# An attention-and-MLP block on one core: the order of the first normalizations, and which loads wait for which work

## The chip, the cores and the metric

The kernel runs on one core of one Trainium2 chip. The metric is device time of one execution in microseconds (us); lower is better. Engines are named as in the profile: PE (TensorE, matrix products), DVE (VectorE), ACT (ScalarE), POOL (GpSimd), SP (SyncE, which here issues every DMA).

## The reference

x is 2048 rows of 1024 in bf16. It is normalized once (mean and variance of each row, no scale or shift) and feeds two branches.

```python
xn = layernorm(x)                              # [2048, 1024]
# branch A: attention, 32 heads of 32
q, k, v = split(xn @ wqkv)
s = softmax(q @ k.T * 32**-0.5) @ v            # per head
s = merge_heads(s) @ wo
# branch B: a second layernorm, an MLP 1024 -> 3584 -> 1024, a gate
y = layernorm(xn)
h = gelu(y @ w1 + b1)                          # tanh form
g = silu(h @ w2 + b2)
return x + s * g
```

## The kernel before

Rows of x are handled in 16 tiles of 128 ("tile t"). A small planner stands in front of the kernel: every instruction is added to it with an engine, an assumed duration, the data it reads and writes, and a priority; a list scheduler (`_Plan.run`) then simulates the engines with those assumptions and fixes one order of instructions for each engine. Lower priority numbers go first; equal ones go in the order in which they were added. After that nothing is dynamic: each engine executes its list in order and waits on semaphores where data come from elsewhere. SP's list is one queue: a DMA that waits holds all that stand behind it. PE's list holds scores, products with V and all "dense" matmuls (projections, MLP, output), so a dense matmul that waits for data also holds the scores behind it.

The opening, about the first 45 us:

- `load_x` (L640) loads the tiles; 0 to 3 come first, then the first wqk slices (`load_qk`, L646: keys, then queries, of the first group of four heads), then tiles 4 to 11. Tiles 12 to 15 and the V weights `wv` wait until tile 4 has been normalized.
- Statistics: DVE's BN_STATS in two halves of 512 columns (L839) and an aggregation (L841); for tiles 1 and 3 ACT does it instead in two passes with an accumulator (L825), and DVE finishes them (L828, L830, L833). DVE adds epsilon (L846), POOL raises to the power -0.5 (L848).
- `normalize` (L796) writes the normalized tile (L798). Tiles 0 to 3 and tile 5 are then transposed by PE (L782) and copied out of PSUM by ACT (L786); all others by a DMA transpose on SP (L802). The result is `xnT`.
- Key, query and V matmuls (L632) follow tile by tile; their casts from PSUM are L769, L740, L753, L730, L718 on DVE and L770, L756 on ACT.
- `filler` matmuls on the identity (L682) keep PE busy while it has nothing else.

From the first key and query tiles on, attention runs in units. A unit is one block of 256 queries and 256 keys for four heads: 8 score matmuls (L904) into PSUM, two exponentials of 128x1024 on ACT (L913; L1248 in the last two half blocks) and 8 products with V (L627). The sums of the exponentials are made on DVE by pairwise additions (L1300, L1303 at first, then L930, L944). There are 512 units, and so 1024 exponentials. The exponentials are written into slots `P`, and in the opening also into the storage of tensors not yet in use (`w1r`, `w2r`, `hT`, one slice each of V and QKT); a tensor's own load then has to wait until those slots have been read.

The MLP runs in the gaps, in 8 chunks of 256 rows. `make_y` (L1065) loads two tiles of x again (L1068), normalizes them (L1070) and transposes them by DMA (L1073); `load_w1` (L1052) brings 256 columns of W1 (512 KB) into a ring of three slots; a "W1 tile" is 16 matmuls on one such slot, an evacuation with the bias b1 on DVE (L1096) and its share of the gelu (L1121 to L1130, tanh on ACT, L1127). W2 loads (L1061, 448 KB) go through a ring of four; the second product is evacuated with b2 (L1148), the gate's tanh is L1155, the result goes to a scratch in DRAM (L1160). `mlp` (L1188) walks through this sequence. `proj` (L1023) loads the weights of the next head group and queues its projections. Attention outputs go to DRAM (L1287) and come back for the output product.

b1 (3584 values) is loaded as a 128x28 tile by one DMA whose rows are single 2-byte elements (L881); b2 is broadcast to 128 partitions (L882). Both wait for the last step of the statistics on POOL (L880).

Planner settings that the change touches: `lead` (a dense item is urgent when its due unit is less than `lead` units ahead of the next score unit), and `seeds`, one number for each 30 us of planned time; a seed other than 0 perturbs the choices in that stretch.

Of the kernel before, what the change touches and what calls it, by code (L numbers as in the profile page):

```python
# [8 lines left out]
BF16 = mybir.dt.bfloat16  # L9
# [23 lines left out]
class _Plan:  # L33
# [3 lines left out]
    def __init__(self):  # L37
        self.ops = []
        self.last_w = {}
        self.readers = {}  # L40
        self.s_queue = []
        self.pv_queue = []
        self.dense = {"pro": [], "q0": [], "v0": [], "tr": [], "last": [], "proj": [], "mlp": [], "w2": [], "wo": []}
        self.lead = 3
        self.filler, self.fill, self.fill0 = None, 0.6, 1400.0
        self.seeds, self.seg, self.amp, self.jit, self.w2b = (), 30000.0, 4.0, 0.1, 20.0
# [421 lines left out]
def bass_recurrent_scan__mha_block__mixer_channel_mlp__prompt_kernel(  # L468
# [27 lines left out]
        0, 0, 234914347, 0, 0, 0, 0, 0, 0, 0, 0, 0, 0, 0, 0, 0, 0, 0, 0, 0, 0, 0, 0, 0, 0, 0, 0, 0, 0,  # L496
# [3 lines left out]
    with ExitStack() as st:  # L500
# [28 lines left out]
        b1T = sb("b1T", [128, FB], BF16)  # L529
# [32 lines left out]
        xnb = [gw[:, i * 1024:(i + 1) * 1024] for i in range(4)]  # L562
        iota_i = utw[:].rearrange("p a b -> p (a b)")[:, 0:256].bitcast(I32)
# [76 lines left out]
        def load_x(t, extra=()):  # L640
            dma(f"x{t}", lambda e: e.dma_start(xst[t], x2[t * 128:(t + 1) * 128, :]), 262144, [], [XS(t)],
                rate=390.0, prio=2, occ=500, lat=2450, extra=extra)
# [18 lines left out]
        for t in range(NTR, 12):  # L661
            load_x(t)
        pool(lambda e: e.iota(iota_i, pattern=[[1, 128]], base=0, channel_multiplier=-1), 300, [], [("ut", 0)])
# [130 lines left out]
        first = {}  # L794

        def normalize(t, rs):  # L796
            def nf(e):
                return e.tensor_scalar(xnb[t % 4], xst[t], mv[:, t, 0:1], lnp[:, t, 1:2], op0=ALU.subtract, op1=ALU.mult)  # L798
            rw = ([XS(t), ("mv", t), rs], [("xnb", t % 4)], 1)
            first[t] = pool(nf, 1150, *rw) if t in PN else dve(nf, c_b4(1024) + 118, *rw)  # L800
            if t >= NTR and t not in TRP:
                dma(f"tr{t}", lambda e: e.dma_start_transpose(xnT[:, :, t * 128:(t + 1) * 128], xnb[t % 4]), 262144,  # L802
                    [("xnb", t % 4)], [("xnT", t, c) for c in range(DC)], prio=0, rate=300.0, occ=1300, lat={4: 2800, 6: 2400, 7: 2000}.get(t, 1000))
# [10 lines left out]
        for n in range(NPR):  # L814
# [6 lines left out]
            for ts in groups:  # L821
# [13 lines left out]
                for t in ts:  # L835
                    if t in AT:
                        continue
                    for c in range(2):
                        dve(lambda e, t=t, c=c: e.bn_stats(stats[:, t, c, :], xst[t][:, c * 512:(c + 1) * 512]),  # L839
                            605, [XS(t)], [("st", t, c)], 1.2)  # L840
                    dve(lambda e, t=t: e.bn_aggr(mv[:, t, :], stats[:, t, :, :].rearrange("p c s -> p (c s)")),  # L841
                        110, [("st", t, 0), ("st", t, 1)], [("mv", t)], 0.95)
                lo, hi = ts[0], ts[-1] + 1
                rs = ("rs", lo)
                if ts[0] not in AT:
                    dve(lambda e, lo=lo, hi=hi: e.tensor_scalar_add(lnp[:, lo:hi, 0], mv[:, lo:hi, 1], EPS), 80,  # L846
                        [("mv", t) for t in ts], [("ve", lo)], 0.95)
# [21 lines left out]
        for n in range(NPR // 2):  # L869
            plan.dense["v0"].append(v_half(0, n, "pro", 0.2 + 0.01 * n))  # L870
            plan.dense["v0"][-1].hold = 6 + 2 * n

        rss = [("rs", t) for t in range(4)] + [("rs", 2 * n) for n in range(2, NPR)]
# [178 lines left out]
        def load_w1(p):  # L1052
            gi, pi = p % NW1R, p % NW1
            src = B_w1[:, pi * 256:(pi + 1) * 256].rearrange("(c p) f -> p c f", p=128)
            dma(f"w1{gi}", lambda e: e.dma_start(w1r[:, gi], src), 524288, [], [("w1", gi)], lat=3100.0)
# [9 lines left out]
        def make_y(c):  # L1065
            for t2 in range(2):
                t = 2 * c + t2
                dma(f"yx{t2}", lambda e, t=t, t2=t2: e.dma_start(yst_t[t2][:], x2[t * 128:(t + 1) * 128, :]), 262144, [],  # L1068
                    [("yst", t2)], rate=390.0, extra=[w1_ev[4]] if c == 1 else ())
# [118 lines left out]
        def mlp(u0, u1):  # L1188
# [378 lines left out]
```

## Time and profile before

| | us |
|---|---|
| median of 3 runs | 1031.92 |
| lowest and highest of them | 1029.39, 1032.52 |
| the profiled execution's own time | 1031.42 |
| its span, first to last instruction | 1029.6 |
| clock granted to PE over the span | 0.999 of full |

The span is measured inside the execution; the time around it (here 1.8 us) belongs to the launch. The costliest groups of instructions of the whole span, with the number of executions, busy time and mean of one, and the engine's idle time before them:

| line, engine | what | count | busy us | mean ns | idle us before |
|---|---|---|---|---|---|
| L913 ACT | exponential, into P | 988 | 921.3 | 1228 | 0.8 |
| L632 PE | W1 product | 1792 | 227.7 | 273 | 0.4 |
| L632 PE | W2 product | 1792 | 223.8 | 273 | 2.0 |
| L930 DVE | addition of exponentials, into PA | 173 | 210.0 | 1217 | 28.4 |
| L944 DVE | addition of those | 173 | 209.7 | 1213 | 1.4 |
| L904 PE | scores | 4032 | 200.2 | 273 | 8.7 |

Instructions of one engine overlap in these records: a mean of 1228 ns does not mean that one begins every 1228 ns, and the spacing has to be read from starts on the timeline. Idle time of an engine that is not the bottleneck costs nothing.

### The profile page before, as it was taken

How to read it: one execution, taken by the hardware profiler on the slowest of the kernel's cores; microseconds unless marked ns; L12 is line 12 of the kernel's file. 1: busy time of each engine (PE TensorE's matmuls, PEld its weight loads, DVE VectorE, ACT ScalarE, POOL GpSimd, SP SyncE). 2: the span in 40 equal slices, each digit the busy share in tenths (PEclk: the TensorE clock that was granted, in tenths of full speed). 3: DMA queues.
4: the chain of work that ended last, by engine and by line, in shares of the span. 5: the costliest groups of instructions: out<-in, count | busy, mean ns of one | idle time of the engine just before them, and what ended most of it. 6: DMA issues, size and time to landing. Idle time of an engine off the chain costs nothing.

```text
span 1029.6 us, 31985 instructions
## 1 busy us (share of the span) xinstructions
PE 1004.2 (98%) x14355; PEld 635.9 (62%) x14355; DVE 956.8 (93%) x1365; ACT 1016.6 (99%) x1087; POOL 11.8 (1%) x21
## 2 busy tenths in 40 slices
PE   8999999999999999999999999999999999999997
PEld 7566656666766576666665676665666665564443
DVE  8899999899899998998899999998999889978987
ACT  8999999999999999999999999999999999999997
POOL 2200000000000000000000000000000000000000
PEclk9999999999999999999999999999999999999999
DMA  8867845745764767446556575556355753873331
GB/s 221 153 154 201 206 123 167 207 110 136 206 187 129 196 189 201 129 134 195 142 146 190 154 215 159 158 173 174 88 150 166 218 161 88 274 230 120 108 93 64
DMA packets 317146, 167.77 MB, mean 163 GB/s; under 512 B 55632, under 2 KB 304976, under 8 KB 317008
## 3 DMA queue, kind: packets, MB, share of 16 engines
q1 hardware_dynamic: 317008, 165.71, 58.2%
q8 instruction: 113, 1.85, 0.8%
q14 instruction: 25, 0.20, 0.1%
HBM read 146.55 MB, written 12.06 MB: 154 GB/s over the span
## 4 chain that ended last, share of the span: by engine, by line
ACT 78%; PE 10%; DVE 7%; DMA 4%; issue 1%; POOL 0%; SPq 0%
ACT P L913 71%; PE ps L632 7%; ACT ut L1127 4%; DMA w2r<-in_B_w_dram 3%; PE ps L904 2%; DVE stats L839 1%; PE ps L627 1%; ACT P L1248 1%; DVE PA L930 1%; ACT gw L1155 1%; DVE PR L944 1%; DMA xnT<-gw 1%; DVE gw L798 1%; ACT w2r L913 1%; DMA hT<-in_A_x_dram 0%
## 5 line engine op out<-in xcount | busy, mean ns | idle before, releaser
L913 ACT ACTIVATE P<-ps 128x1024 bf16<-128x1024 f32 x988 | 921.3, 1228 | 0.8 <-PE ps L904 0.7
L930 DVE TENSOR_TENSOR PA<-P 128x2048 bf16<-128x2048 bf16 x173 | 210.0, 1217 | 28.4 <-ACT P L913 27.7
L632 PE MATMUL ps<-yT,w1r 128*128 128x256 bf16 x1792 | 227.7, 273 | 0.4 <-DVE QKT L730 0.3
L632 PE MATMUL ps<-w2r,hT 128*128 128x256 bf16 x1792 | 223.8, 273 | 2.0 <-DMA w2r<-in_B_w_dram 1.2
L944 DVE TENSOR_TENSOR PR<-PR,PA 128x2048 bf16<-128x2048 bf16 x173 | 209.7, 1213 | 1.4
L904 PE MATMUL ps<-QKT 32*128 32x256 bf16 x4032 | 200.2, 273 | 8.7 <-ACT P L913 6.2
L632 PEld LDWEIGHTS ps<-yT,w1r 128*128 128x128 bf16 x1792 | 163.8, 98 | 53.1 <-issue 29.1
L632 PEld LDWEIGHTS ps<-w2r,hT 128*128 128x128 bf16 x1792 | 163.0, 98 | 52.4 <-issue 30.6
L904 PEld LDWEIGHTS ps<-QKT 32*128 32x128 bf16 x4032 | 59.7, 92 | 138.2 <-ACT P L913 130.0
L627 PE MATMUL ps<-P,V 128*32 128x256 bf16 (+1 forms) x4080 | 137.6, 272 | 0.0
L632 PE MATMUL ps<-xnT,wqk 128*128 128x512 bf16 (+2 forms) x584 | 132.2, 354 | 2.4 <-DMA xnT<-gw 1.0
L627 PEld LDWEIGHTS ps<-P,V 128*32 128x32 bf16 x4080 | 95.3, 96 | 33.2 <-issue 24.0
L632 PE MATMUL ps<-wv,xnT 128*128 128x256 bf16 (+2 forms) x704 | 87.8, 264 | 1.6 <-DMA xnT<-gw 1.0
L632 PEld LDWEIGHTS ps<-xnT,wqk 128*128 128x128 bf16 x584 | 49.9, 98 | 51.7 <-issue 15.2
L1096 DVE TENSOR_TENSOR hT<-ps,b1T 128x512 bf16<-128x512 f32 x112 | 76.8, 685 | 4.4 <-PE ps L632 4.0
L930 DVE TENSOR_TENSOR PR<-P 128x2048 bf16<-128x2048 bf16 x60 | 72.8, 1214 | 0.0
L632 PEld LDWEIGHTS ps<-wv,xnT 128*128 128x128 bf16 x704 | 55.8, 98 | 23.9 <-issue 10.8
L1127 ACT ACTIVATE ut<-ut 128x3072 bf16<-128x3072 bf16 (+2 forms) x27 | 59.6, 2206 | 0.0
L730 DVE CAST QKT<-ps 128x512 bf16<-128x512 f32 x58 | 39.7, 685 | 1.5 <-PE ps L632 1.1
L999 DVE STREAM_TRANSPOSE nt<-ps 128x256 f32<-128x256 f32 x63 | 27.9, 444 | 14.0 <-PE ps L627 13.9
L1121 DVE TENSOR_TENSOR ut<-hT 128x2048 bf16<-128x2048 bf16 (+1 forms) x37 | 35.3, 957 | 0.1
L1130 DVE TENSOR_TENSOR hT<-ut,hT 128x2048 bf16<-128x2048 bf16 (+1 forms) x37 | 35.0, 951 | 0.0
(116 smaller groups left out, 587.8 us busy)
## 6 DMA issues: line engine op xcount, KB each, us to landing
w1r<-in_B_w_dram SPq DMA_DIRECT2D x112, 512.0 KB, 4.4
w2r<-in_B_w_dram SPq DMA_DIRECT2D x128, 448.0 KB, 4.5
yst<-in_A_x_dram SPq DMA_DIRECT2D x18, 256.0 KB, 4.5
wqk<-in_A_wqkv_dram SPq DMA_DIRECT2D x16, 256.0 KB, 3.7
g_scratch<-gw SPq DMA_DIRECT2D x32, 128.0 KB, 3.3
hT<-in_A_x_dram SPq DMA_DIRECT2D x14, 256.0 KB, 3.9
o_scratch<-ot SPq DMA_DIRECT2D x56, 64.0 KB, 3.4
xnT<-o_scratch SPq DMA_DIRECT2D x7, 512.0 KB, 6.4
```

Source lines behind the costliest of these rows:

```text
L627: ins = e.matmul(dst(j), lhsT=lhsT(j), rhs=rhs(j), start=start, stop=stop, tile_position=(0, 32 * j), skip_group_check=True)
L632: return e.matmul(dst, lhsT=lhsT, rhs=rhs, start=start, stop=stop, skip_group_check=True)
L730: dve(lambda e: e.tensor_copy(QKT[sl][:, which, tq * 512:(tq + 1) * 512], bank(it.bank)), c_ps(512), [], [(nm, sl, 2 * tq), (nm, sl, 2 * t ...
L904: ins = e.matmul(bank(b0[j], kk * 256, (kk + 1) * 256), lhsT=QKT[sl][32 * j:32 * j + 32, 1, kb * 128:(kb + 1) * 128], rhs=QKT[sl][32 * j:3 ...
L913: x = act(lambda e, h=h: e.activation(Pt[pi][:, 2 * h:2 * h + 2].rearrange("p j k q -> p (j k q)"), ps[:, pr[h] * 1024:(pr[h] + 1) * 1024] ...
L930: return dve(lambda e: e.tensor_tensor(dst[:].rearrange("p u j q -> p (u j) q"), src[:].rearrange("p u j k q -> p (u j) k q")[:, :, 0, :], ...
L944: return dve(lambda e: e.tensor_tensor(fl3(pr), fl3(pr), fl3(PA[i]), op=ALU.add), c_b16(2048), [("PA", i), tok], [tok], 3.2)
L999: dve(lambda e: e.transpose(nt_t[:], bank(pv.bank, 256, 512)), c_ps(256) + 120, [], [("nt",)], prio, pv)
L1096: w1_ev[p] = dve(lambda e: e.tensor_tensor(hT[:, hs], bank(it.bank).rearrange("p (k t) -> p k t", k=2), b1T[:, 2 * pi:2 * pi + 2].unsqueez ...
L1121: dve(lambda e, u_=u_, x_=x_: e.tensor_tensor(u_, x_, x_, op=ALU.mult), c_b16(n), hs_, [("ut", ui)], gp)
L1127: act(lambda e: e.activation(ua, ua, ACT.Tanh, scale=GC), c_acts(run * 512), uts, uts, ga)
L1130: dve(lambda e, u_=u_, x_=x_: e.tensor_tensor(x_, u_, x_, op=ALU.mult), c_b16(n), [("ut", ui)] + hs_, hs_, gp)
```

## The change

It has these parts.

1. `normalize` gets priority 0.8 instead of 1 for tiles 0 to 3, which puts it ahead of statistics (1.2), aggregation, epsilon and the small steps of tiles 1 and 3 (0.95). The planner's assumed durations change for BN_STATS (605 to 620 ns) and the epsilon step (80 to 110), and its assumed rate for the loads of tiles 2 and 3.
2. b1 is no longer loaded element by element. POOL clears a 128x32 corner of the `ut` storage, four DMAs bring 28 rows of 32 values each into it, after the load of tile 11, and one DVE transpose makes `b1T`, after the last normalization.
3. b2 is loaded after the fifth W1 tile has been evacuated, instead of after the statistics.
4. Loads wait for later work. The next group's key slice waits until the transpose of tile 15 has landed (before: until tile 15 was normalized), and so does the MLP's first load of x (before: free). The query slice of that group waits for the exponentials of unit (2, 7), the key slice of group 2 for the third W1 tile, W1 tile 1 for the exponentials of unit (2, 5), and W1 tile 2 for those of unit (2, 7). Units are named (query block, key block).
5. `lead` goes from 3 to 5, and the one seed that was not 0 becomes 0.

```diff
-        self.lead = 3
+        self.lead = 5
...
-        0, 0, 234914347, 0, 0, 0, 0, 0, 0, 0, 0, 0, 0, 0, 0, 0, 0, 0, 0, 0, 0, 0, 0, 0, 0, 0, 0, 0, 0,
+        0, 0, 0, 0, 0, 0, 0, 0, 0, 0, 0, 0, 0, 0, 0, 0, 0, 0, 0, 0, 0, 0, 0, 0, 0, 0, 0, 0, 0,
...
-        b1T = sb("b1T", [128, FB], BF16)
+        b1T = sb("b1T", [128, 32], BF16)
...
+        b1c = utw[:, 7, 480:512]
...
-                rate=390.0, prio=2, occ=500, lat=2450, extra=extra)
+                rate=230.0 if t in (2, 3) else 390.0, prio=2, occ=500, lat=2450, extra=extra)
...
+        pool(lambda e: e.memset(b1c, 0.0), 150, [], [("b1c", k) for k in range(4)], 0)
+        for k in range(4):
+            dma(f"b1{k}", lambda e, k=k: e.dma_start(b1c[32 * k:32 * k + FB, :], B_b1.rearrange("(q b p) -> b q p", b=4, p=32)[k]),
+                2048, [], [("b1c", k)], prio=2)
...
-            rw = ([XS(t), ("mv", t), rs], [("xnb", t % 4)], 1)
+            rw = ([XS(t), ("mv", t), rs], [("xnb", t % 4)], 0.8 if t < NTR else 1)
...
-                dma(f"tr{t}", lambda e: e.dma_start_transpose(xnT[:, :, t * 128:(t + 1) * 128], xnb[t % 4]), 262144,
+                trs[t] = dma(f"tr{t}", lambda e: e.dma_start_transpose(xnT[:, :, t * 128:(t + 1) * 128], xnb[t % 4]), 262144,
...
-                            605, [XS(t)], [("st", t, c)], 1.2)
+                            620, [XS(t)], [("st", t, c)], 1.2)
...
-                    dve(lambda e, lo=lo, hi=hi: e.tensor_scalar_add(lnp[:, lo:hi, 0], mv[:, lo:hi, 1], EPS), 80,
+                    dve(lambda e, lo=lo, hi=hi: e.tensor_scalar_add(lnp[:, lo:hi, 0], mv[:, lo:hi, 1], EPS), 110,
...
+        dve(lambda e: e.transpose(b1T[:], b1c), c_b16(32) + 60, [("b1c", k) for k in range(4)], [("b1",), ("ut", 1)], 2.5, None, [first[NT - 1]])
...
-        dma("b1", lambda e: e.dma_start(b1T[:], B_b1.rearrange("(fb p) -> p fb", p=128)), 8192, [("s3",)], [("b1",)], lat=5500)
-        dma("b2", lambda e: e.dma_start(b2b[:], B_b2.rearrange("(o d) -> o d", o=1).to_broadcast([128, D])), 262144,
-            [("s3",)], [("b2",)], occ=2900)
...
-            wk = load_qk(hg, 1, [first[NT - 1]] if hg == 1 else ())
-            wq = load_qk(hg, 0)
+            wk = load_qk(hg, 1, [trs[NT - 1]] if hg == 1 else [w1_ev[2]] if hg == 2 else ())
+            wq = load_qk(hg, 0, [got[(2, 7)][0]] if hg == 1 else ())
...
-                    [("yst", t2)], rate=390.0, extra=[w1_ev[4]] if c == 1 else ())
+                    [("yst", t2)], rate=390.0, extra=[w1_ev[4]] if c == 1 else [trs[NT - 1]] if c == 0 else ())
...
-                    load_w1(s_[1] * NW1 + s_[2])
+                    load_w1(s_[1] * NW1 + s_[2], [got[(2, 5)][0]] if s_[1] == 0 and s_[2] == 1 else [got[(2, 7)][0]] if s_[1] == 0 and s_[2] == 2 else ())
...
+                    if s_[1:] == (0, 4):
+                        dma("b2", lambda e: e.dma_start(b2b[:], B_b2.rearrange("(o d) -> o d", o=1).to_broadcast([128, D])), 262144,
+                            [], [("b2",)], occ=2900, extra=[w1_ev[4]])
```

More of the change, by code (lines that the diff above doesn't have):

```diff
@@ L792, in bass_recurrent_scan__mha_block__mixer_channel_mlp__prompt_kernel @@
         pro_q, q0_q = plan.dense["pro"], plan.dense["q0"]
-        first = {}
+        first, trs = {}, {}
         def normalize(t, rs):
@@ L1050, in bass_recurrent_scan__mha_block__mixer_channel_mlp__prompt_kernel, with load_w1 @@
         w1_ev = {}
-        def load_w1(p):
+        def load_w1(p, extra=()):
             gi, pi = p % NW1R, p % NW1
             src = B_w1[:, pi * 256:(pi + 1) * 256].rearrange("(c p) f -> p c f", p=128)
-            dma(f"w1{gi}", lambda e: e.dma_start(w1r[:, gi], src), 524288, [], [("w1", gi)], lat=3100.0)
+            dma(f"w1{gi}", lambda e: e.dma_start(w1r[:, gi], src), 524288, [], [("w1", gi)], lat=3100.0, extra=extra)
         def load_w2(q, r, extra=()):
```

## The prediction

> **What bounds the kernel now.** The page comes first: the span, the busy shares, and the chain of work that ended last.
>
> ```profile
> span 1029.6 us, 31985 instructions
> ...
> PE 1004.2 (98%) x14355; PEld 635.9 (62%) x14355; DVE 956.8 (93%) x1365; ACT 1016.6 (99%) x1087; POOL 11.8 (1%) x21
> ...
> ACT 78%; PE 10%; DVE 7%; DMA 4%; issue 1%; POOL 0%; SPq 0%
> ```
>
> ACT and PE are both nearly full, and ACT carries the chain. An average does not say where a change can still win, so next the busy time by stretch (columns: stretch, its length, busy us of PE, PEld, DVE, ACT, POOL, clock, DMA share, GB/s):
>
> ```profile
> 60.00:70.00 10.00, 9.20 (x147) 5.52 (x144) 9.37 (x17) 10.00 (x12) 0.00 (x0) 1.00 0.26 73
> ...
> 100.00:120.00 20.00, 19.92 (x301) 13.29 (x299) 19.75 (x29) 20.00 (x23) 0.00 (x0) 1.00 0.80 206
> 120.00:150.00 30.00, 29.57 (x400) 17.69 (x398) 29.91 (x45) 30.00 (x32) 0.00 (x0) 1.00 0.65 175
> 150.00:200.00 50.00, 49.38 (x702) 34.29 (x702) 47.46 (x62) 50.00 (x54) 0.00 (x0) 1.00 0.60 168
> ```
>
> ACT has no gap there. Is it full of work, or stretched? On its timeline 22 exponentials take 20.17 us start to start, 0.917 each. From 54.47 to its last exponential's end at 1022.36 (967.9 us) it runs 984 of them (1024 less the 40 before), 902.0 us, 27 tanh of the gelu (10 of 2.65, 9 of 1.80, 8 of 0.945: 50.3) and 16 of the gate (0.945: 15.1). The sum, 967.4, leaves 0.5 us lost in 968. So the span is the time at which ACT becomes gapless, plus fixed work, plus a tail of 7.2 us. What can be won lies in ACT's timeline of the first 46 us (start, length, engine, line, operation, idle before it and who ended it):
>
> ```profile
> 11.75 0.40 ACT L770 ACTIVATE QKT<-ps 128x256 bf16<-128x256 f32 x1
> 12.54 1.02 ACT L786 ACTIVATE xnT<-ps 128x1024 bf16<-128x1024 bf16 x1 [0.39 <-PE ps L782]
> 13.46 1.02 ACT L913 ACTIVATE P<-ps 128x1024 bf16<-128x1024 f32 x1
> ...
> 21.85 0.51 ACT L756 ACTIVATE QKT<-ps 128x256 bf16<-128x256 f32 x1
> 22.87 3.77 ACT L913 ACTIVATE P<-ps 128x1024 bf16<-128x1024 f32 x4 [0.51 <-PE ps L904]
> ...
> 29.29 1.94 ACT L913 ACTIVATE QKT<-ps 128x1024 bf16<-128x1024 f32 x2 [0.76 <-PE ps L904]
> ...
> 42.31 1.94 ACT L913 ACTIVATE w1r<-ps 128x1024 bf16<-128x1024 f32 x2
> 45.42 3.77 ACT L913 ACTIVATE w1r<-ps 128x1024 bf16<-128x1024 f32 x4 [1.18 <-PE ps L904]
> ```
>
> Four gaps, 0.39, 0.51, 0.76 and 1.18: 2.84 us in all. (Earlier ones wait for x tiles, whose loads stay.) The largest is traced back: the scores of L904 at 44.98 stood in PE's order behind the V matmuls, which waited twice for "DMA xnT<-gw", the transposes of tiles 14 and 15. Landing times of the transposes, first those of tiles 12 and 13, then 14 and 15:
>
> ```profile
> L802 SPq DMA_TRANSPOSE xnT<-gw x2: 1232/1270/1307, 34.8 to 36.1; - x2
> ...
> DMA to landing us min/median/max: 2.7/2.8/2.8
> ```
>
> ```profile
> L802 SPq DMA_TRANSPOSE xnT<-gw x2: 1231/1270/1308, 38.1 to 39.4; - x2
> ...
> DMA to landing us min/median/max: 5.1/5.3/5.5
> ```
>
> The same transfer takes twice as long. What follows it in SP's queue:
>
> ```profile
> 40.76 0.58 SPq L650 DMA_DIRECT2D wqk<-in_A_wqkv_dram  x1
> 41.38 2.44 SPq L1068 DMA_DIRECT2D yst<-in_A_x_dram  x2
> ```
>
> These three loads of 256 KB are what the change holds back until the last transpose has landed.
>
> **Part by part.** The built order of both kernels gives the positions, rows of before the durations; what follows is arithmetic on those.
>
> *Normalizations first (priority 0.8), with the new rates and statistics costs.* DVE rows of before:
>
> ```profile
> 8.21 0.54 DVE L798 TENSOR_SCALAR gw<-hT,mv,lnp 128x1024 bf16<-128x1024 bf16 x1
> 9.19 0.55 DVE L798 TENSOR_SCALAR gw<-hT,mv,lnp 128x1024 bf16<-128x1024 bf16 x1 [0.44 <-POOL lnp L848]
> ...
> 12.34 0.41 DVE L769 CAST QKT<-ps 128x256 bf16<-128x256 f32 x1
> ...
> 28.94 0.42 DVE L753 CAST QKT<-ps 128x256 bf16<-128x256 f32 x1 [1.18 <-PE ps L632]
> ```
>
> In the new order tile 1 is normalized ahead of two small steps (L846 of tile 2, L828 of tile 3, at 8.07 and 8.15), so near 8.0. Tile 2's epsilon step then comes after it, at about 8.45, POOL's power needs 0.78 and some 0.2 around it: 9.43 instead of 9.19. Tile 3 follows two statistics (0.61 each) at about 11.45 instead of 11.33. From 9.19 to 27 us DVE works almost without a gap, so I carry 0.24 us of loss through it. The cast of Q (L769) now follows tile 3's normalization directly, 11.93 instead of 12.34; scores at 12.42 instead of 12.82, the first exponential at 12.9 instead of 13.46. But it takes the place that the copy of tile 3 (L786) had on ACT: that goes from 12.54 to 13.8, the K cast behind it from 14.36 to 15.6, the second scores from 14.82 to 16.05. ACT idles 0.75 (12.15 to 12.9) and about 0.55 (15.95 to 16.5) where it idled 0.39. Against that, one exponential now stands behind the cast of K at 21.85 and covers the scores that cost 0.51. ACT at 26 us: 1.30 idle instead of 0.90, 0.4 later.
>
> That 0.4 is eaten by the gap of 0.76, which stays: it waits for tile 7's transpose (landed near 27.8), issued behind the same statistics. It moves by DVE's 0.24. So ACT stands at 29.5 instead of 29.29: **0.24 lost**. Bounds: 0.76 + 0.51 + 0.39 = 1.66 won if tile 7 lands that much earlier, 0.7 lost if PE meets every one of the delays in turn.
>
> *The last transposes alone.* DVE reaches tile 15's normalization (38.35) 0.24 late, plus what the cast of K at 28.94 adds: the new order puts it one statistics step (0.6) earlier, so DVE idles up to 0.6 longer there. I take 0.5: transpose 15 issued at about 39.9 and, with nothing behind it, landing 2.8 later at 42.7 (before: 39.4 + 5.5 = 44.9). Eight V matmuls (0.47) and one of K (0.13) lie between, scores at 43.3, exponentials possible from 43.8. ACT gets there only at 44.24 + 0.24: the 1.18 is gone. The next key casts need 1.05 of matmuls and 0.42 of cast each, and each unit of scores gives ACT 1.83 of cover. **1.18 won**. Bounds: 1.18 if landing is below 3.9, or 1.0 lost if it remains 5.5 (scores at 46.0).
>
> *b1 in four loads, b2 later.* SP idles from 9.99 to 15.19, and four issues of 0.43 (the old b1's) lie in there. The memset on POOL in front of the iota costs 0.1 (as its memsets do), hidden by 47 filler matmuls; the new transpose of b1 on DVE is 128x32, at most the 0.44 of the 128x256 one of L999, in a stretch where ACT has cover. b2's 2.92 of issue moves behind the fifth W1 tile, where SP waits 4.4 us (82.5 to 86.93) anyway. Without that cover, 2.9 late on one W1 load. **0**.
>
> *wqk, W1 and x later.* The wait on transpose 15 holds all of SP: behind it are x, its transposes and W1. The x loads go from 41.4 to about 43.5, land by 48.2 at their 4.6, and DVE normalized them at 47.49. First W1 matmul: after 25 units of scores before, after 28 now, about 66.3. W1 tile 1 waits for unit 22's exponentials (unit 16 began at 45.42, 1.83 each, less the gain: 57.3), lands with the page's 4.4 near 62 and is used near 68; tile 2 waits for unit 24, near 61, and behind wqk lands near 66.5, used near 70.2. Margins 6 and 3.7: **0**, bounds 0 and 5.0 lost (the last rival).
>
> *Lead 5, seed 0.* They reorder PE and DVE through the middle; the last 4346 of PE's 14358 matmuls stand as before, so the tail is the same. **0**; lost 0.5 in 968 before, so nothing to win.
>
> Sum: +0.24 - 1.18 = -0.94. The profiled execution took 1031.42 (span 1029.6 and 1.8 around it), 0.50 below the median 1031.92. From it: 1030.5; from the median: 1031.0. I take **1030.6**.
>
> **The rivals.**
> *All early gaps close*: the DMA is freer, tile 7 also lands sooner, the first exponential is not followed by a gap. For: first scores come 0.4 earlier. Against: tile 7's transpose has the same loads (wv, x14, x15) before it. 1031.42 - 2.84 = 1028.6.
> *The transposes stay slow.* For: tile 9's transpose at 27.15 landed after 4.57 with no load beside it, as the chain shows (27.15 4.57). Against: the busy DMA engines and 83 GB/s from 41 to 42, just when loads join. Then the delays of DVE are paid: 45.4 landing, scores 46.0, exponentials 46.5 instead of 45.42: +1.1, 1032.5. [...]
> *DVE falls behind (slower).* DVE has 0.25 us free of 20 from 100 to 120 and 0.09 of 30 to 150. The MLP starts three units later, and its first W2 matmul stands behind 79 units of scores instead of 71: 8 units, at 3.3 units per W1 tile 2.4 tiles late. A tile costs DVE 0.69 of evacuation and 1.3 of gelu (145.6 us of L1121, L1122, L1123, L1129, L1130 over 112): 2.0, so 5.0 us pushed into the full stretch. It decides once ACT waits for DVE to free a P slot: 1031.42 - 0.94 + 5.0 = 1035.5. For: the rows above. Against: Q, K and V casts come forward into the space, and 150 to 200 has 2.5 free.
>
> **How the numbers follow.** Forecast 0.42, all gaps 0.22, slow transposes 0.16, DVE behind 0.20. 0.3% is 3.1 us: 1028.8 to 1035.0. Faster: 0.6 of the second and a seventh of the first (medians scatter by 1.5) 0.19. Slower: most of the fourth, a little of the third, 0.21. Same 0.60. Range 1028.2 to 1034.4; the forecast's own is 1029.5 to 1031.9.
>
> **What would show it.** Landing of transposes 14 and 15 near 2.8; no gap on ACT between 30 and 50; first exponential near 12.9 with a second gap near 16; a gap near 28.5 still there; no ACT wait from 50 to 900. Wrong if 14 and 15 still land at 5, or if ACT waits for DVE after 60.

## The result, and the profile after

The changed kernel takes 1033.71 us (median of 7, 1030.9 to 1035.78) against 1030.78 for the kernel before on the same chip: ratio 1.0031, interval 1.002 to 1.0042. Run again twice, it gave 1.0017 (1.0007 to 1.0028) and 1.0013 (1.0004 to 1.0021). So it is slower by 0.13 to 0.31%, where 1030.6, a gain, was forecast.

The profiled execution does not look slower. The page after (span, busy shares, chain by engine):

```profile
span 1029.0 us, 31986 instructions
...
PE 1002.3 (97%) x14350; PEld 636.8 (62%) x14350; DVE 956.4 (93%) x1366; ACT 1016.3 (99%) x1087; POOL 11.7 (1%) x22
...
ACT 86%; PE 7%; DVE 3%; DMA 2%; issue 0%; POOL 0%; SPq 0%
```

Its span is 0.6 shorter than before. ACT's timeline in the opening (start, length, engine, line, operation, idle before it and who ended it; the exponentials of L913 are now L916):

```profile
12.35 1.02 ACT L916 ACTIVATE P<-ps 128x1024 bf16<-128x1024 f32 x1 [0.59 <-PE ps L907]
...
15.98 1.02 ACT L916 ACTIVATE P<-ps 128x1024 bf16<-128x1024 f32 x1 [0.50 <-PE ps L907]
...
28.00 2.11 ACT L916 ACTIVATE QKT<-ps 128x1024 bf16<-128x1024 f32 x2
...
41.01 1.94 ACT L916 ACTIVATE w1r<-ps 128x1024 bf16<-128x1024 f32 x2
43.81 2.99 ACT L916 ACTIVATE w1r<-ps 128x1024 bf16<-128x1024 f32 x3 [0.86 <-PE ps L907]
```

From 43.81 on ACT has no gap in the opening any more, 1.61 earlier than before; the gap near 28.5 is gone, one of 0.86 is left of the 1.18. Of these 1.61 the span keeps 0.6: the stretch from there to the last exponential is 0.13 longer, and what follows it takes 8.1 instead of 7.2. The transposes of tiles 14 and 15 (the profile's view of these two instructions):

```profile
L807 SPq DMA_TRANSPOSE xnT<-gw x2: 1307/1308/1309, 36.8 to 38.1; - x2
DMA to landing us min/median/max: 3.6/4.0/4.5
```

They land in 3.6 and 4.5, not in 2.8. On PE (timeline), the V matmuls wait for them twice:

```profile
40.40 0.23 PE L633 MATMUL ps<-wv,xnT 128*128 128x128 bf16 x1 [0.56 <-DMA xnT<-gw]
...
42.70 0.62 PE L633 MATMUL ps<-wv,xnT 128*128 128x128 bf16 x8 [1.24 <-DMA xnT<-gw]
```

The reader is to see what this profile is not: it was taken of the shortest of the seven executions (1030.9 us, mean PE clock 0.999). The other six took 1033.5 to 1035.8, at mean clocks of 0.996 and 0.997. Over all executions of this kernel in the runs below and here, 14 of 33 have 0.997 or less, of the kernel before 6 of 140. Those 14 take 1034.1 on the mean, the other 19 take 1032.2. What happens in them had to be caught in a trace.

### The profile page after: what moved, and what is told of

Same layout as the page of the kernel before. It is cut to its first block, busy times and chain, and to the rows that moved or that the text cites. A ratio compares the mean times of both kernels' runs of the same rounds, so it can differ in the third digit from the quotient of the medians.

```text
span 1029.0 us, 31986 instructions
## 1 busy us (share of the span) xinstructions
PE 1002.3 (97%) x14350; PEld 636.8 (62%) x14350; DVE 956.4 (93%) x1366; ACT 1016.3 (99%) x1087; POOL 11.7 (1%) x22
## 3 DMA queue, kind: packets, MB, share of 16 engines
q8 instruction: 112, 1.84, 0.8%
## 4 chain that ended last, share of the span: by engine, by line
ACT 86%; PE 7%; DVE 3%; DMA 2%; issue 0%; POOL 0%; SPq 0%
ACT P L916 78%; PE ps L633 5%; ACT ut L1130 4%; PE ps L907 1%; ACT gw L1158 1%; DMA w2r<-in_B_w_dram 1%; ACT P L1254 1%; PE ps L628 1%; DMA xnT<-gw 1%; DVE PA L933 1%; DVE PR L947 1%; ACT w2r L916 1%; ACT PA L830 0%; ACT xnT L791 0%; DVE stats L844 0%
## 5 line engine op out<-in xcount | busy, mean ns | idle before, releaser
L916 ACT ACTIVATE P<-ps 128x1024 bf16<-128x1024 f32 x988 | 921.4, 1237 | 1.5 <-PE ps L907 1.5
L628 PEld LDWEIGHTS ps<-P,V 128*32 128x32 bf16 x4080 | 95.7, 96 | 31.1 <-issue 21.4
```

The costliest lines, as they stand in the source:

```text
L628: ins = e.matmul(dst(j), lhsT=lhsT(j), rhs=rhs(j), start=start, stop=stop, tile_position=(0, 32 * j), skip_group_check=True)
L916: x = act(lambda e, h=h: e.activation(Pt[pi][:, 2 * h:2 * h + 2].rearrange("p j k q -> p (j k q)"), ps[:, pr[h] * 1024:(pr[h] + 1) * 1024] ...
```

## The experiments

Three theories at first. T1: a hole of PE in the opening lowers the clock granted to it. T2: the later loads of W1 and W2 make ACT wait in the middle. T3: the tail is longer. Ratios are to the kernel before, on the chip of that run; "low" counts executions with a mean clock of 0.997 or less.

### First batch: holes filled

The trace after shows PE idle for 1.27 us at 13.1 (the copy of tile 3 now stands behind the first exponential on ACT) and the waits near 40 to 43 above. `a_again` is the changed kernel once more; `fillA` fills the first hole, `fillB` the later ones, `fillAB` both, with matmuls that compute nothing:

```diff
 # fillA, in the key matmuls
+if n == 1 and lo == 0 and dc == DC - 1:
+    for _ in range(18):
+        ins = e.matmul(bank(b, 256, 384), lhsT=ident[:], rhs=ident[:], ...)
 # fillB, between V matmuls of tiles 12 to 15
+if last and dc == DC - 1 and t4 in (1, 2):
+    for _ in range(8 if t4 == 1 else 18):
+        ins = e.matmul(bank(b, 384, 512), lhsT=ident[:], rhs=ident[:], ...)
```

Expected of `a_again`:

> The changed kernel once more, unaltered, to see its spread and to get a trace of a typical execution: its first trace (1030.9 us, clock 0.999) was the fastest of seven, the other six took 1033.5 to 1035.8 with a mean granted clock of 0.996 to 0.997. Theory 1 (clock): in typical executions the granted PE clock falls for some us in or just after the opening, where PE now has holes (1.27 us at 13.1, 1.02 at 22.7, 0.56 and 1.24 between 39.8 and 42.7); the trace then shows a window below 1.00 between 13 and 50 us, the exponentials become gapless 2 to 5 us later than in the first trace (43.8), and the rest is as there. Theory 2 (middle): the clock is at 1.00 in the opening and ACT waits between 60 and 900 us for PE, behind late W1 or W2 loads, by 2 to 5 us in sum. Theory 3 (tail): the last exponential ends near 1020.9 as in the first trace and the tail takes 10 to 13 us instead of 8.1.

Expected of `fillA`:

> The changed kernel with 18 more filler matmuls (about 1.1 us of PE) in the hole at 13.1 us, all orders as they are. Theory 1, if this hole trips the clock: about 1030.5, clock 0.999 in nearly all executions. Theory 1 with another hole, theory 2 or theory 3: as the changed kernel, about 1033.7.

Expected of `fillB`:

> The changed kernel with 8 and 18 more filler matmuls in front of the V matmuls of tiles 14 and 15, in the two holes between 39.8 and 42.7 us, all orders as they are. Theory 1, if these holes trip the clock: about 1030.5, clock 0.999. Otherwise about 1033.7.

Expected of `fillAB`:

> Both fillings. Theory 1: about 1030.5, clock 0.999, whichever of the two holes it is. Theories 2 and 3: about 1033.7, clock 0.997 unchanged.

| | median us | ratio | low |
|---|---|---|---|
| a_again | 1032.91 | 1.0017 (1.0007 to 1.0028) | 3 of 12 |
| fillA | 1031.49 | 0.9999 (0.999 to 1.0008) | 0 of 11 |
| fillB | 1031.39 | 1.0005 (0.9996 to 1.0014) | 1 of 11 |
| fillAB | 1032.2 | 1.0012 (1.0004 to 1.0021) | 0 of 11 |

Every filler seemed to help against the low clocks, which looked like T1. That does not follow: all three also change how many instructions stand on PE ahead of what follows, which the second batch did not yet consider. And fillAB, without one low clock, is still slower than the kernel before (1.0012), so the clock is not the whole loss. T2 was seen in part, in a_again's trace (PE's and SP's timelines):

```profile
199.16 0.50 PE L633 MATMUL ps<-w2r,hT 128*128 128x256 bf16 x3 [1.25 <-DMA w2r<-in_B_w_dram]
```

```profile
192.46 1.31 SPq L1163 DMA_DIRECT2D g_scratch<-gw  x2
193.81 0.56 SPq L1293 DMA_DIRECT2D o_scratch<-ot  x1
194.41 5.26 SPq L1064 DMA_DIRECT2D w2r<-in_B_w_dram  x3
```

A load of W2 stands behind three stores in SP's queue and comes late; ACT then idles 1.03 at 200.04. The trace after has 0 there, and 0.36 at 913.

### Second batch: the hole doubled, single parts undone

```diff
 # hole42: the 42 filler matmuls at 17.5 us are left out
+if 66 < nfill["n"] <= 108:
+    return None
 # early: SP no longer waits for transpose 15
+for o in plan.ops:
+    if trs[NT - 1] in o.deps and o.eng == "SP":
+        del o.deps[trs[NT - 1]]
 # fillA_sp: fillA, and one W2 load ahead of three stores
+held, load = sp[i:i + 3], sp[i + 3]
+sp[i:i + 4] = [load] + held
 # e_prio: part 1 of the change undone
-rw = ([XS(t), ("mv", t), rs], [("xnb", t % 4)], 0.8 if t < NTR else 1)
+rw = ([XS(t), ("mv", t), rs], [("xnb", t % 4)], 1)
...
```

Expected of `hole42`:

> The changed kernel without the 42 filler matmuls that TensorE runs at about 17.5 us (they compute nothing that is used); everything else stands as it was. So a second hole of about 2.4 us follows the one of 1.27 us at 13.1 us. Theory T1 (a hole in the opening makes the chip grant a lower TensorE clock): more executions than the 9 of 19 of the changed kernel, nearly all, show a mean granted clock of 0.997 or less, the trace shows a stretch behind the hole with a clock clearly under 1.00, and the median is 2 to 4 us over the changed kernel's 1033, 1035 to 1037. Rival (the clock of 0.996 to 0.997 has another origin than holes in the opening): the share stays near one half and the median stays at 1033, within 1.

Expected of `early`:

> The changed kernel with the wait of the queue on the landing of transpose 15 taken away: the key slice of wqk and the first MLP x tiles are issued right behind transpose 15, in the same order; b2, W1 and the four small loads of b1 stay as in the change. Theory of the prediction (the transposes are slow because loads run beside them): transposes 14 and 15 land in about 5 us again instead of 3.6 and 4.5, and ScalarE is gapless from 1 to 2 us later than 43.8 to 44.1 (the times of the changed kernel's two traces), so the time is 1 to 2 us above the changed kernel's at the same clock. Rival (the wait is not what made them faster: they are slow by their place, and the wqk load is not needed early): landings of 3.6 to 4.5 as before and ScalarE gapless at 43.8 to 44.2, no change of time.

Expected of `fillA_sp`:

> fillA (the changed kernel with 18 extra matmuls of about 1.1 us in the hole at 13.1 us) with, in addition, the first load of W2 issued ahead of the two g_scratch stores and the o_scratch store at 192 to 194 us in the queue's order; no other order moves. Theory T2 (what the opening gained is partly given back at 199 us, where TensorE and then ScalarE wait for that load): no wait for W2 near 199 us, ScalarE's gap of 0.59 there (1.03 in the repeat of the changed kernel) gone, and a median 0.6 to 1.0 under fillA's 1031.49, so about 1030.7. Rival (ScalarE's gap there is taken again by a later wait, or the time between runs hides it): 1031.5, within 0.3.

Expected of `e_prio`:

> The changed kernel with the normalizations of the first four tiles back at their old place behind the statistics, and the planner's old durations and rates with them; the deferred loads, the four loads of b1 and the lead stay as changed. Theory T1: the hole of 1.27 us at 13.1 us is gone, the clock is 0.998 or more in nearly all executions, and what is kept is the gain of the late loads alone: 1030 to 1031, 2 to 3 under the changed kernel. Rival (the slowness is in the deferred loads, not in the reordering): 1033, as the changed kernel, with clocks of 0.996 to 0.997 in about half of the executions.

| | median us | ratio | low |
|---|---|---|---|
| hole42 | 1031.27 | 1.0004 (0.9994 to 1.0013) | 5 of 10 |
| early | 1033.27 | 1.0019 (1.0008 to 1.003) | 4 of 7 |
| fillA_sp | 1030.81 | 1.0001 (0.9992 to 1.001) | 0 of 11 |
| e_prio | 1031.35 | 1.0009 (1.0 to 1.0018) | 1 of 11 |

hole42 speaks against T1 as it stood: with a second hole of 2.26 us it is no slower than the changed kernel, but nearer to the kernel before. Its trace, of an execution at 0.999, shows no fall of the clock behind that hole, in a stretch in which PE is busy 52% (busy time of PE, PEld, DVE, ACT, POOL in the stretch, then clock, DMA share, GB/s):

```profile
18.50:21.90 3.40, 1.79 (x22) 1.44 (x23) 3.40 (x11) 3.40 (x5) 1.03 (x2) 1.00 1.08 342
```

None of its five low executions was traced, so falls behind this hole are not excluded.

early brings the loads of wqk and x back beside the last transposes: these land in 4.9 and 4.5, PE waits 2.06 in one piece, and the time is that of the changed kernel. So of the wait for transpose 15, no gain in time can be shown. fillA_sp takes the wait at 199 us away (no gap on ACT there), but its ratio is that of fillA: T2's waits are real, their removal does not show in the time. e_prio's low clocks are rare and its ratio lies between; it, too, has another number of instructions on PE (4 more), so it does not settle part 1.

### Third batch: more traces, to catch an execution with a low clock

Expected of `a_look1`:

> The changed kernel unaltered, to catch one of its executions of 1031.5 us and more in a trace (all traces so far are of its executions with a clock of 0.999 or of one with 0.998). T1 (a lower clock in the opening): where the mean granted clock is 0.997 or less, the record shows a stretch of 0.50 somewhere between 13 and 25 us, behind the hole of 1.27, and the first exponentials come late there. Theory T4 (the lower mean comes from the end: the clock falls one step earlier in the tail, after the last dense matmuls): the stretch of 0.50 begins before 1024 us, the opening is as in the traces so far (ScalarE gapless at 43.8 to 44.1), and the tail behind the last exponential takes more than 8.1. If the execution is again one of 0.998 or more, it shows neither.

Expected of `a_look2`:

> The changed kernel unaltered once more, with the same question and the same two answers as the look before it: at a mean clock of 0.997 or less, 0.50 between 13 and 25 us (T1), or 0.50 from before 1024 us at the end and an undisturbed opening (T4).

Expected of `hole_look`:

> hole42 (the changed kernel without the 42 filler matmuls at 17.5 us) unaltered, to catch one of its executions with a clock of 0.997 or less (5 of 10 so far). T1: a stretch of 0.50 in the record behind its hole of 2.3 us at 17.8, of some 3 us or a multiple, and ScalarE later than in its first trace (last exponential ended 1020.5) by 2 or more. T4: no such stretch, and an early fall at the end.

Expected of `e_prio_sp`:

> e_prio (part 1 undone) with two loads of W2 moved ahead of stores in the queue's order: the one at 194 us ahead of two g_scratch stores and an o_scratch store, and the last one at 909 us ahead of one o_scratch store. In e_prio's trace ScalarE's gaps from these two were 0.81 and 0.61. T2 (loads of W2 behind stores cost what the late loads win): both gaps gone, a median 1.0 to 1.4 under e_prio's 1031.35, about 1030.1, and under the kernel before by 0.5. Rival (other waits take their place): 1031.3, within 0.3.

`a_look1`, `a_look2` and `hole_look` are the changed kernel (twice) and hole42 again; `e_prio_sp` is e_prio with two loads of W2 moved ahead of stores as in fillA_sp. None of these three executions had a low clock (0.998, 0.999, 0.999). e_prio_sp: 1029.83, ratio 0.9997 (0.9987 to 1.0006), 1 of 12 low; the wait at 199 was gone in its trace, that at 913 was not (0.74; 0.61 in e_prio's). Its ratio is 0.0012 below e_prio's, as T2 has it, but the two intervals overlap, so it does not settle T2.

The traces gave something else. In the last burst of matmuls PE stands for 0.94 us in the trace after (1.27 in a_look1, 1.53 in a_look2, 1.21 in early), always ahead of the same matmul:

```profile
1021.28 0.28 PE L628 MATMUL ps<-P,ones 128*32 128x128 bf16 x6
...
1022.50 0.34 PE L628 MATMUL ps<-P,ones 128*32 128x128 bf16 x10 [0.94 <-issue]
```

It waits for "issue", that is for nothing that the profile shows. In the trace 14,338 of the 14,350 matmuls lie ahead of that place, 28,676 instructions with their weight loads. The page after counts the transfers of instructions (queue, packets, MB, share):

```profile
q8 instruction: 112, 1.84, 0.8%
```

1.84 MB in 112 packets is 16 KB each, and the 28,700 instructions counted on PE are 256 for each packet. Between the starts of two such packets PE starts 254 instructions on the mean, in the trace before and in the trace after. So blocks of 256 instructions, one a packet, are an estimate from these counts. By it, 28,676 is 112 times 256 and 4 more: PE stands where block 113 begins, to within four instructions. In the packet records that block's transfer starts 0.47 to 0.77 us after the start of the burst in these traces, takes 0.9 to 1.4 us, and PE goes on 1.3 to 1.5 us after its end. In a_again it started 0.59 before the burst, and there is no stand. The change took 5 matmuls (fillers) out of PE's stream. With the kernel before that block begins 15 matmuls before the end of the burst, its transfer starts 1.4 us before the burst, and PE does not stand (PE's timeline before; the second line waits for DVE, as in every trace):

```profile
1022.77 0.40 PE L627 MATMUL ps<-P,ones 128*32 128x128 bf16 x16
1024.75 0.60 PE L632 MATMUL ps<-yst,xnT 128*128 128x512 bf16 x2 [1.58 <-DVE xnT L1282]
```

This is T5: the place of that block, not the work, makes PE stand.

### Fourth batch: five filler matmuls

```diff
 # a_tail5: the changed kernel, 5 fillers more at 1013 us
+if nfill[0] == 118:
+    n += 5
 # b_tail5: the kernel before, 5 fillers fewer at 1014 us
+if nfill[0] in (119, 121):
+    return None
+if nfill[0] == 123:
+    n = 1
```

`a_best` is a_tail5 with the two loads of W2 ahead of stores; `a_same_chip` is the changed kernel beside them.

Expected of `a_same_chip`:

> The changed kernel unaltered, as the measure for the three beside it on one chip: 1032.5 to 1033.5, with mean clocks of 0.997 or less in about half of the executions, and TensorE's stand of about 1.2 us before the last 10 matmuls of the last burst (4 of 5 traces so far).

Expected of `a_tail5`:

> The changed kernel with 5 more filler matmuls (0.3 us) in TensorE's pause at 1013 us, so that its stream is again as long as that of the kernel before; the opening and all orders stay. T5 (a block of instructions begins inside the last burst): TensorE's stand of 0.94 to 1.53 there is gone, ScalarE's last pause is 3.0 instead of 3.9 to 4.5, the mean clock is 0.998 or more in nearly all executions, and the median is 1.0 to 2.0 under the changed kernel's on this chip. T1 (the hole at 13 us): the hole stands as before, so the clock of 0.997 or less stays in half of the executions and the time with it, within 0.4.

Expected of `b_tail5`:

> The kernel before with 5 filler matmuls fewer at 1014 us; no part of the change is in it. T5: TensorE stands 0.9 to 1.5 us before the last 10 matmuls of the last burst in most executions, ScalarE's last pause grows from 3.0 to about 4.2, mean clocks of 0.997 or less turn up in some tenths of the executions (1 to 2 of 82 so far), and the median is 1.0 to 2.0 above the kernel before. T1: no hole in the opening was made, so no change, within 0.3.

Expected of `a_best`:

> a_tail5 with, in addition, two loads of W2 ahead of stores in the queue's order (as in e_prio_sp: at 194 us ahead of two g_scratch stores and one o_scratch store, at 909 us ahead of one o_scratch store). If T5 and T2 are both right, what is left is the opening's gain: 0.5 to 1.0 under a_tail5, about 1029.5 to 1030, and 0.5 to 1.5 under the kernel before. If T2's waits come back at other places, it is a_tail5's time within 0.3.

| | median us | ratio | low |
|---|---|---|---|
| a_same_chip | 1032.22 | 1.0013 (1.0004 to 1.0021) | 5 of 12 |
| a_tail5 | 1032.14 | 1.0006 (0.9997 to 1.0015) | 3 of 11 |
| b_tail5 | 1032.23 | 1.0004 (0.9995 to 1.0012) | 2 of 11 |
| a_best | 1032.08 | 1.0009 (0.9999 to 1.002) | 5 of 11 |

The stand goes where T5 says. Without any part of the change, the kernel before gets it (b_tail5, PE's timeline):

```profile
1022.81 0.28 PE L627 MATMUL ps<-P,ones 128*32 128x128 bf16 x7
1024.42 0.34 PE L627 MATMUL ps<-P,ones 128*32 128x128 bf16 x9 [1.32 <-issue]
```

and the changed kernel loses it (a_tail5):

```profile
1024.10 0.40 PE L628 MATMUL ps<-P,ones 128*32 128x128 bf16 x16
1026.08 0.60 PE L633 MATMUL ps<-yst,xnT 128*128 128x512 bf16 x2 [1.58 <-DVE xnT L1293]
```

The stand shows in ACT's last pause, 3.9 to 4.5 us in the five traces with it and 3.0 without. In the medians it is worth less than was expected: the ratios move by 0.0007 down and 0.0004 up, 0.4 to 0.7 us, and the intervals overlap, so no gain in time is shown. The low clocks stay. a_best shows no gain from the loads of W2 (a gap of 0.40 at 199 stayed, and PE stood 0.48 in the burst). So T5 is a part at most, not the whole.

The rest came with the traces of this batch: a_same_chip, a_tail5 and a_best were caught with the clock down. a_same_chip, busy time by stretch (columns as above; the eighth is the clock):

```profile
40.30:43.71 3.41, 1.00 (x19) 0.67 (x18) 2.79 (x4) 1.67 (x3) 1.04 (x2) 1.00 0.89 81
43.71:47.13 3.42, 3.42 (x29) 2.18 (x26) 1.36 (x3) 3.26 (x4) 0.00 (x0) 0.50 0.72 216
47.13:50.54 3.41, 3.41 (x33) 1.40 (x32) 3.41 (x7) 2.54 (x4) 0.00 (x0) 1.00 0.04 14
```

and what PE and then ACT do there:

```profile
42.77 0.23 PE L633 MATMUL ps<-wv,xnT 128*128 128x128 bf16 x1 [2.40 <-DMA xnT<-gw]
...
44.45 0.42 PE L633 MATMUL ps<-xnT,wqk 128*128 128x256 bf16 x1
```

```profile
43.38 1.94 ACT L916 ACTIVATE w1r<-ps 128x1024 bf16<-128x1024 f32 x2 [1.74 <-PE ps L907]
45.47 1.94 ACT L916 ACTIVATE w1r<-ps 128x1024 bf16<-128x1024 f32 x2 [0.16 <-PE ps L907]
48.28 1.02 ACT L916 ACTIVATE w1r<-ps 128x1024 bf16<-128x1024 f32 x1 [0.87 <-PE ps L907]
```

Here the two waits are one of 2.40, because transpose 14 landed late (5.2 instead of 3.6); PE is busy 29% of a stretch of 3.41 us, and in the next 3.41 us it has half its clock. That costs ACT three gaps in place of one. The same in a_tail5 (wait 1.99, busy 42%) and a_best (2.21, 35%). The same group of 32 exponentials near 100 us starts at 102.10, 101.63 and 102.19 in these three, and at 99.33 to 100.05 in the five traces of the changed stream without it (after, a_again, a_look1, a_look2, early): 2.2 us later. early is the one to compare with: its wait of 2.06 is longer than a_tail5's, but it lay across two of the stretches of 3.41 us on whose grid the three falls begin and end (last section), and PE was busy 55% of the one that held most of it. The clock did not fall, and its group starts at 99.99. The trace after has, in its stretch before 44.1:

```profile
40.69:44.10 3.41, 2.17 (x36) 1.40 (x29) 2.42 (x4) 2.55 (x4) 0.00 (x0) 1.00 0.08 16
```

64%, and no fall. So T1 holds in another place than supposed.

### Fifth batch: why the transposes are late

No load of wqk, W1 or x runs beside transposes 14 and 15 in the changed kernel. The packet records show two transfers of instructions there, of 8 KB and of 16 KB on two other queues. Times in us; "slowest packet" is that of a transpose, whose packets mostly take 18 ns; "PE busy" is the share in the stretch of 3.41 us around the wait:

| trace | 8 KB from | 16 KB from | slowest packet | landing 14, 15 | PE busy | clock next |
|---|---|---|---|---|---|---|
| before | 39.88 | 41.70 | 2.24 | 5.5, 5.1 | 0.71 | 1.00 |
| after | 38.61 | 40.21 | 0.21 | 3.6, 4.5 | 0.64 | 1.00 |
| a_again | 38.95 | 40.43 | 1.47 | 3.5, 4.5 | 0.56 | 1.00 |
| early | 38.16 | 39.81 | 1.35 | 4.9, 4.5 | 0.55 | 1.00 |
| a_tail5 | 38.77 | 40.32 | 1.39 | 4.8, 4.3 | 0.42 | 0.50 |
| a_best | 39.51 | 40.81 | 1.36 | 5.0, 4.5 | 0.35 | 0.50 |
| a_same_chip | 38.69 | 40.32 | 1.76 | 5.2, 4.7 | 0.29 | 0.50 |
| hole42 | 40.04 | 43.12 | under 0.2 | 3.4, 2.9 | 0.85 | 1.00 |

This is T6: the 16 KB transfer, whose start moves with the length of PE's stream ahead of it, runs into the transposes (39.81 to 40.81 in the six traces of the changed opening in the table); in hole42, 42 matmuls shorter there, it comes at 43.12, behind them. Where no packet is slow, packets still wait: in the trace after, the last 22 packets of transpose 15 start when the 16 KB are over, at 41.24.

The first batch already held a test of T6. The 18 matmuls of fillA bring the 16 KB to 37.33, and then transposes 12 and 13, which land in 2.7 and 2.9 in every trace of the changed kernel, are the slow ones (fillA; 14 and 15 take 4.3 and 3.3):

```profile
L811 SPq DMA_TRANSPOSE xnT<-gw x2: 1232/1276/1319, 35.0 to 36.2; - x2
DMA to landing us min/median/max: 4.6/4.7/4.8
```

How many land late goes with when the 16 KB start, counted from the issue of transpose 14: 2.76 to 2.98 us later in the four traces of the changed opening in which 14 and 15 are both late (a_same_chip, a_tail5, a_best, early), 3.27 to 3.47 in the four in which 15 alone is (after, a_again, a_look1, a_look2). The kernel before does not fit this (3.57, and both late); there loads of wqk and x are issued from 40.76 on, and no run tells their part from that of the 16 KB.

`a_wide` moves the 16 KB without a hole:

```diff
 # a_wide: the 42 fillers as 11 wide ones and a half, as long in all
+if 66 < nfill[0] <= 108:
+    if nfill[0] % 4 == 2 or nfill[0] == 108:
+        w = 256 if nfill[0] == 108 else 512
+        return e.matmul(bank(b, 0, w), lhsT=ident[:], rhs=xnT[:, 0, 0:w], ...)
+    return None
```

(By the built order these are 10 of 512 columns and one of 256, 31 matmuls fewer.) `a_wide_sp` adds the two loads of W2 ahead of stores.

Expected of `a_wide`:

> The changed kernel with the 42 filler matmuls at 17.5 us made as 11 of 512 columns and the last of 256 (as long in all, some 2.5 us, no hole; they compute nothing that is used). TensorE's stream is 31 matmuls shorter from there on; all orders stay. T6 (the 16 KB fetch of instructions slows transposes 14 and 15): the fetch of 39.8 to 41.8 comes at about 42.5, transposes 14 and 15 land in 2.8 to 3.6 (3.5 to 5.2 in the changed kernel), TensorE's waits for them shrink from 1.6 to 2.4 in sum to under 0.8, mean clocks of 0.997 or less are gone, the block that began in the last burst is gone from it (ScalarE's last pause 3.0), and the median is 1.5 to 2.5 under the changed kernel's 1032 to 1033.5, about 1030.3, not slower than the kernel before. Rival (they are slow by their place, or by each other): landings of 3.5 to 5.2 stay, clocks of 0.997 or less in a third to a half of the executions, and about 1032.

Expected of `a_wide_sp`:

> a_wide with the two loads of W2 ahead of stores in the queue's order, as in e_prio_sp and a_best. With T6 and T2 right: 0.3 to 1.0 under a_wide, about 1029.7, and under the kernel before by 0.8 to 1.5. With T6 right and T2's waits back at other places: a_wide's time within 0.3.

| | median us | ratio | low |
|---|---|---|---|
| a_wide | 1030.5 | 0.9993 (0.9983 to 1.0003) | 2 of 12 |
| a_wide_sp | 1030.12 | 0.9988 (0.9979 to 0.9998) | 1 of 12 |

In a_wide's trace the 16 KB start at 42.33, and transposes 14 and 15 land so; below it PE's only wait for them, and ACT:

```profile
L815 SPq DMA_TRANSPOSE xnT<-gw x2: 1232/1274/1316, 37.8 to 39.0; - x2
DMA to landing us min/median/max: 3.0/3.2/3.5
```

```profile
41.27 0.23 PE L633 MATMUL ps<-wv,xnT 128*128 128x128 bf16 x1 [0.57 <-DMA xnT<-gw]
```

```profile
41.88 5.61 ACT L924 ACTIVATE w1r<-ps 128x1024 bf16<-128x1024 f32 x6
```

Landing 3.5 and 3.0, one wait of 0.57 instead of two of 1.80 together, no gap on ACT from 36 to 50 us, no stand in the last burst. Against the changed kernel's 1.0013 to 1.0031 the ratio falls by 0.002 to 0.004, 2.1 to 3.9 us; as both effects go at once, their shares are not told apart. The lateness has moved, not vanished: the 16 KB ahead of these start at 31.1, and transposes 10 and 11 land in 4.2 and 3.8 instead of 2.7 and 2.8, where ACT has a gap of 0.32. The loads of W2 on top are worth 0.4 in the median, within the scatter; a_wide_sp is the one version whose interval lies below the kernel before, by 0.02 to 0.21%.

## Why the prediction was wrong, point by point

Without a fall of the clock the opening gained about what was forecast or more (ACT is gapless from 43.55 to 44.27 in four traces of the changed kernel, from 45.42 and, in b_tail5, 45.03 without the change), but by other terms than the forecast's. What turned the sign are two costs that the sum put at nothing: the clock behind PE's waits, and the place of the blocks of instructions.

**The bound.** Right for the middle: ACT sets the time there. From its gapless start to its last exponential the trace after needs 977.07 us, before 976.94. The tail, taken as fixed, was not.

**Normalizations first, +0.24.** Wrong sign in the traces of the changed kernel without a fall of the clock. The first exponential came at 12.35 (12.9 in the text), the second gap near 16 as forecast, but tile 7's keys came early too and the gap of 0.76 closed: ACT stood at 28.00, not at 29.5. In the trace before, tile 7's transpose stood behind the issue of tile 6's, which held SP for 2.40 us; in the trace after that took 1.56, so it is SP that let tile 7 through, not DVE, which had normalized it at 21.4 and at 21.1. Why the issue is shorter is open. The first rival came true in part: 1.95 of gaps are left, 2.84 before. This term was -1.29 (28.00 against 29.29).

**The last transposes alone, -1.18.** The step that failed is "with nothing behind it, landing 2.8 later". With nothing behind them they landed in 3.5 to 5.2, and with loads behind them, in early, no later (4.9, 4.5). The partner in the changed kernel is the 16 KB transfer of instructions: with it at 37.33 (fillA) transposes 12 and 13 are late (4.6 to 4.8), and where it comes behind 14 and 15 they land in 3.4 and 2.9 (hole42, 43.12) and in 3.5 and 3.0 (a_wide, 42.33). This term was 0.32 won (a gap of 0.86 instead of 1.18), not 1.18, so that the sum of the two, -1.61 where -0.94 was forecast, is right in sign by luck. The second rival ("The transposes stay slow") had the landings right, but its price of 1.1 on ACT was not paid in the trace after. The clue was in it: tile 9's transpose, slow "with no load beside it", had a 16 KB transfer beside it from 29.7 on, and in the trace after, where it was issued at 26.0 and that transfer began at 28.6, it landed in 2.9. A reading is wrong as well: 5.5 belongs to tile 14, and tile 15 landed after 5.1, at 44.5 and not at 44.9. What goes with the late landings is a transfer on another queue: in six traces of the table a packet of these transposes took 1.35 to 2.24 us beside a 16 KB transfer, where most take 18 ns.

**What the waits cost.** The sum had no term for the clock. In the unlucky case the waits join into one of 2.0 to 2.4, PE runs at a clock of 0.50 for 3.41 us, and ACT is 2.2 us later. If the 14 of 33 executions with a low mean clock are those, this is 0.9 on the mean. The mean clock is only a proxy: the three traced cases had 0.996, 0.997 and 0.998.

**"Lead 5, seed 0": nothing.** "The last 4346 of PE's 14358 matmuls stand as before, so the tail is the same": the order is, the place of the blocks of instructions is not. Five matmuls fewer ahead of it make PE stand 0.94 to 1.53 in 5 of the 6 traces of this stream, and the trace after takes 8.1 behind its last exponential instead of 7.2. In the medians of the tests no more than 0.4 to 0.7 shows, within the scatter.

**b1, b2, W1, x later, 0.** The one wait seen for them in the trace after, 0.4 of DVE for x, does not reach ACT, and DVE did not fall behind (the last rival). What grew are ACT's gaps from loads of W2 behind stores: one of 0.17 in the trace before, in those of the changed kernel 0 to 1.03 at 199 us and up to 0.99 at 913. Why they differ between executions is open.

With the two effects of the instruction transfers out of the way, a_wide's 0.9993 is 0.7 below the kernel before, where the forecast's sum was 0.94 below. Its interval reaches 1.0003, so that the opening's gain was there and was taken back is likely, and shown only in the traces. Open: why the distance between transpose 14 and the 16 KB differs between executions; whether loads beside the transposes cost anything once the 16 KB are moved (no run has both); whether part 1 alone is worth anything, since undoing it also changes the stream's length; and the low clocks of hole42, of a_wide's two executions and of a_wide_sp's one, which no trace shows.

## What to carry to other kernels

Count the instructions that an edit adds or takes away on PE, not only their order: transfers of instructions stand among the DMA's packets, and a few matmuls more or fewer (5 to 42 here) moved one into or out of a transpose or a burst. When a hole is filled to test a theory, the stream becomes longer too; test the two apart. A profile shows one execution: where clocks or times of the others differ from it, take further traces until one of those is caught.

## What the runs showed of the hardware

- The clock granted to PE is 1.00 or 0.50 in the records. The falls to 0.50 in the opening of a_same_chip, a_tail5 and a_best filled the stretches 43.71:47.13, 42.51:45.92 and 43.36:46.77, 3.42, 3.41 and 3.41 us, with 1.00 ahead of them and behind. In before and after the record stands at 1.00 for 1020.585 us and then at 0.50 to its end; 299 steps of 3.413 us make that length. The step is an estimate from these lengths; counted in it from the start of a trace's clock record, the three falls begin and end on the grid. What went with a fall was the busy share of PE in the stretch ahead of it: 0.29, 0.35 and 0.42 were followed by 0.50; 0.52 (hole42), 0.55 (early) and 0.56 (a_again) were not. Stretches at the end of the span agree: 0.45 (a_same_chip, from 1023.3) was followed by 0.50, 0.46 (after, from 1020.3) and 0.48 (a_best, from 1023.0) were not. The longest wait of PE ahead of one of the three falls was 2.40 us (a_same_chip).
- The transfers of instructions on q8 are packets of 16 KB, 113 in before and 112 in after, for 28,710 and 28,700 instructions counted on PE: 254 and 256 for each, and 254 on the mean between the starts of two packets in both. Blocks of 256 are an estimate from this. With five matmuls fewer ahead of it PE's stand came (1.32, b_tail5), with five more it went (a_tail5; in a_best, with the same five, PE stood 0.48 fifteen matmuls before the end of the burst). The transposes of 128x1024 that were late beside such a transfer landed in 3.8 to 5.2 us in the versions of the changed kernel, the others in 2.7 to 3.6, and PE went on 1.3 to 1.5 us after its end where it stood.
